# Retention and a SwiGLU block on one core: shorter tick queues, a later first split batch, narrower first weight loads

## The chip, the cores and the metric

The kernel runs on one core of one Trainium2 chip. A core has five engines with a queue each: TensorE (PE, matrix products; PEld is its weight load), VectorE (DVE), ScalarE (ACT), GpSimd (POOL) and SyncE (SP, which here only issues DMAs). Each engine takes its own queue in order; semaphores hold an instruction until what it needs is there. ScalarE's queue carries DMA issues too. The metric is the device time of one execution in microseconds; five executions of the kernel before were timed.

## What is computed

```python
scores = (q @ k^T) / sqrt(64)                      # batch 8, heads 8, sequence 576, head size 64
gamma  = 1 - 2 ** (-5 - h)                         # one decay per head h
ret    = scores * where(i >= j, gamma ** (i - j), 0)
x      = (ret @ v), laid out as 4608 tokens x 512  # heads side by side
g, val = x @ w_gate, x @ w_val                     # 512 -> 1536
out    = (silu(g) * val) @ w_out                   # 1536 -> 512
```

q, k and v are 32-bit floats. The three weight matrices are 64-bit floats in memory, so the kernel loads eight bytes per element and turns them into 32-bit floats itself.

## The kernel before

**Retention.** Two heads of one batch entry make a pair; there are 32 pairs, four per batch entry (HP = 4). The sequence of a pair is cut in nine chunks of 64. Within a chunk the masked scores are applied to v (`own_values`, L519); what earlier chunks contribute goes through a 64 x 64 state per chunk (`new_states`, L529; the decayed running sums in `masked`, L565 to L587) that the queries then read (`earlier_values`, L540 and L544). `to_x` moves the result to the token matrix.

**Ticks.** The pairs run as a software pipeline. `tick(t)` issues for pair t the transposes, for pair t-1 the scores (L552, L558), new states and masks, and for pair t-2 the two value steps and the move to x. TensorE's part of a tick is issued at once; what other engines do is put as small functions into a list `pieces`, and `part_on` hands one of them out at a time between the products of the feed-forward block. `go_on(len(pieces))` at the head of a tick hands out all that is left. For a light tick (decays folded into the queries in advance) the list of before is: `copies` with `outputs`; `own`; then `pairs`, `odd`, `evens`, one at a time; `keys` with the scaling of the queries; the transpose of the queries (qT); that of the keys (kT, both L483 on VectorE); and the next load.

**The first four pairs** (t = 0 to 3) are transposed on TensorE instead, against the identity matrix: for each of q and k four 128 x 128 transposes into a bank (L468) and, for the ninth chunk, two 64 x 64 transposes ("tails") into bankC (L470); two copies (L472, L473) bring them to SBUF, by VectorE for pair 0 and by ScalarE after it.

**Weights.** A weight load `load_w(m)` (L383, L385) brings a 1 MB block of 64-bit numbers into one of three places (RAWS = 3). `split(j)` makes two 32-bit parts of half a block on ScalarE (L402, L403), and issues a later `load_w` once both halves of a block are read; `rounding(j)` joins them on VectorE (L416, L417), and issues `split(j + 1)`.

**Feed-forward.** The first 512 tokens are computed directly: `up0` (L715) makes gate and value for one of 12 blocks of 128 hidden columns, `down0` (L727) the output. The other 4096 tokens are four tiles of 1024, each by a bilinear scheme with fewer block products: 3 x 26 `up_step`s (L941) and 26 `down_step`s (L982) per tile, with sums of operands before and of results after them (L749, L883, L911, L957 to L964). In the first of these tiles (n = 1) the weight sums are still being formed, on GpSimd and ScalarE, and each is stored to DRAM by a DMA on ScalarE's queue (L945); later tiles fetch them back, on SP (L844), into a ring of eight places. `up_step` hands out one piece where its result has fewer than five operations, `down_step` three.

**What sets the order.** The order on each engine is that of the Python program (a manual schedule); no planner changes it. In the 52 steps of n = 1 after its first 26, six ticks (12 to 17) are spread evenly by `merge`; four more lie in its 26 down steps.

Of the kernel before, what the change touches and what calls it, by code (L numbers as in the profile page):

```python
# [154 lines left out]
def kernel(  # L155
# [34 lines left out]
    B, H, S, D = q.shape  # L190
    NT, DM = out.shape
    DF = moe_w_gate.shape[1]
    P = 128
    HP = H // 2
# [3 lines left out]
    CW = NFULL * P  # L198
# [22 lines left out]
    bankA, bankB, bankC, bankE = banks = [ps.tile([P, 512], F32, name=n) for n in ("bankA", "bankB", "bankC", "bankE")]  # L221
# [138 lines left out]
    for u in range(NF // 2):  # L360
        for gv, w in enumerate((moe_w_gate, moe_w_val)):
            src = w[:, u * 2 * P : (u + 1) * 2 * P].rearrange("(c p) n -> p c n", p=P)
            weights.append((src, [w_up[:, u // 2, gv, 2 * (u % 2) + f].rearrange("p k x -> p (k x)") for f in range(2)]))
    NUP = len(weights)
    for u in range(NF // 2):
        src = moe_w_out[u * 2 * P : (u + 1) * 2 * P, :].rearrange("(f p) n -> p f n", p=P)
# [4 lines left out]
    RAWS = 3  # L371
    raws, parts = {}, {}

    def load_w(m, parts=range(2)):

        i, queue = order[m], nc.sync if m < 5 else nc.scalar
        raw = rest[:, raw_at + m % RAWS * 2048 : raw_at + (m % RAWS + 1) * 2048]
        raws[i] = raw.bitcast(I32)
        dst, src = raw.bitcast(I64), weights[i][0]
        if i < NUP:  # L380
            dst = dst.rearrange("p (c n) -> p c n", n=2 * P)
            for cols in [ts(f, P) for f in parts] if m < 2 else (slice(0, 2 * P),):
                queue.dma_start(out=dst[:, :, cols], in_=src[:, :, cols])  # L383
        else:
            queue.dma_start(out=dst.rearrange("p (f n) -> p f n", f=2), in_=src)  # L385
# [7 lines left out]
    def split(j):  # L393

        i, f = halves[j]
        bits = bits_of(i, f)
        top, ulp = [rest[:, part_at + 512 * (2 * n + j % 2) : part_at + 512 * (2 * n + j % 2 + 1)] for n in range(2)]  # L400
        blocks = lambda a: a.rearrange("p (c m) -> p c m", m=P)
        nc.scalar.activation(out=blocks(top), in_=bits[:, :, :, 1].bitcast(F32), func=AF.Prelu, scale=2.0 ** -112, alpha=2.0 ** 32)  # L402
        nc.scalar.activation(out=blocks(ulp.bitcast(I32)), in_=bits[:, :, :, 0].bitcast(U32), func=AF.Copy, scale=2.0 ** -29)  # L403
        parts[j] = top.bitcast(I32), ulp.bitcast(I32)
        m = j + 1 if 1 < j < 4 else j // 2 + RAWS
        if f and m < len(order):
            load_w(m)

    def rounding(j):

        i, f = halves[j]
        dst = weights[i][1][f].bitcast(I32)
        top, ulp = parts.pop(j)
        nc.vector.tensor_scalar(out=dst, in0=top, scalar1=3, scalar2=None, op0=ALU.logical_shift_left)  # L416
        nc.vector.tensor_tensor(out=dst, in0=dst, in1=ulp, op=ALU.add)  # L417
        if j + 1 < len(halves):
            split(j + 1)
# [36 lines left out]
    def transposes(i):  # L456
        p = i % HP
        qk, kn, vt = loaded.pop(i)
        qT = early[i] if i < HP else qp.tile([P, S], F32, tag="qT", name="qT")
        st[i] = dict(qT=qT, kn=kn, v=vt)  # L460
        pieces = []

        copy = nc.scalar.copy if i else nc.vector.tensor_copy
        if i < HP:

            for n, (t, src, bank) in enumerate(((kT, kn, bankB), (qT, qk, bankA)) if i else ((qT, qk, bankA), (kT, kn, bankB))):
                for c in range(NFULL):
                    nc.tensor.transpose(bank[:, ts(c, P)], src[:, ts(c, P)], ident)  # L468
                for hl in range(2):
                    nc.tensor.matmul(bankC[half[hl], ts(n, L)], src[half[hl], CW : CW + D], ident[half[hl], half[hl]],  # L470
                                     start=True, stop=True, skip_group_check=True)
                copy(t[:, 0:CW], bank)  # L472
                copy(t[:, CW:S], bankC[:, ts(n, L)])  # L473
        else:
            if light(i):
                def scale_q():

                    src = qk[:, 0].rearrange("p (j r) d -> p r j d", r=2)
                    for r in range(2):
                        nc.scalar.activation(out=src[:, r], in_=src[:, r], func=AF.Copy, scale=piece[:, 2 * p + r : 2 * p + r + 1])  # L480
                pieces.append(scale_q)
            for n, t in enumerate((qT, kT)):
                pieces.append(lambda n=n, t=t: nc.vector.transpose(out=t, in_=qk[:, n].rearrange("p j d -> p (j d)")))  # L483

        every = slice(0, P)

        def keys():
            blocks = kn.rearrange("p (g d) -> p g d", d=D)
            if i < HP:
                parts = [(0, every, blocks[:, 0 : NC - 1 : 2]), (1, every, blocks[:, 1:NC:2]), (1, half[1], blocks[half[1], NC - 1])]  # L490
            elif whole(i):
                parts = [(0, every, blocks[:, 0:NFULL]), (1, every, blocks[:, NFULL:NC])]
            else:
                parts = [(hl, every, blocks[:, hl : 2 * NFULL : 2]) for hl in range(2)]
            for hl, rows, at in parts:
                scale = key[rows, 2 * p + hl : 2 * p + hl + 1]
                if vector(i) or 1 < i < HP:
                    (nc.vector if vector(i) else nc.gpsimd).tensor_scalar(out=at, in0=at, scalar1=scale, scalar2=None, op0=ALU.mult)
                else:
                    nc.scalar.activation(out=at, in_=at, func=AF.Copy, scale=scale)  # L500

        if light(i):
            return [lambda: (keys(), pieces[0]())] + pieces[1:]
        return [keys] + pieces
# [138 lines left out]
    def tick(t, lo=HP, hi=NP, spread=False, then=None):  # L643
        go_on(len(pieces))
        if hi == HP:

            if lo <= t - 1 < hi:
                scores(t - 1, True)
                new_states(t - 1)
                pieces.extend(masked(t - 1))  # L650
                go_on(3)
            if t + 1 == HP:
                split(0)
                rounding(0)
            if lo <= t - 2 < hi:
                own_values(t - 2)
            for f in transposes(t) if lo <= t < hi else ():
                f()
            if t + 1 == HP:
                rounding(1)  # L660
            if lo <= t - 2 < hi:
                earlier_values(t - 2)
                to_x(t - 2)[0]()
            return
        if lo <= t - 2 < hi:
            own_values(t - 2)
        if lo <= t - 1 < hi:
            new_states(t - 1)
        if lo <= t - 2 < hi:
            earlier_values(t - 2)  # L670
        if lo <= t - 1 < hi:
            scores(t - 1, t - 2 < lo)
        if lo <= t - 1 < hi and whole(t - 2) and not whole(t - 1):
            decay(slice(0, H), slice(0, H), half[1])
        copies, *masks = masked(t - 1) if lo <= t - 1 < hi else (lambda: None,)
        keys, *new = transposes(t) if lo <= t < hi else (lambda: None,)
        outputs = to_x(t - 2)[0] if lo <= t - 2 < hi else lambda: None
        late = needed(1) - 4 <= t < needed(1) - 2 or light(t - 2)
        if late:
            pieces.append(lambda: (copies(), outputs()))  # L680
        else:
            pieces.extend([lambda: (copies(), keys()), outputs])
        pieces.extend(masks)
        if late:
            pieces.append(keys)
        pieces.extend(new)
        if then:
            pieces.append(then)
        if not spread:
            go_on(len(pieces))  # L690

# [18 lines left out]
    def up0(f, chunks):  # L710

        pair = banks[2 * (f % 2) : 2 * (f % 2) + 2]
        for gv, bank in enumerate(pair):
            for c in chunks:
                nc.tensor.matmul(bank, w_up[:, f // 4, gv, f % 4, c // 2, (c % 2) * P : (c % 2 + 1) * P], xs[0][:, c, :],  # L715
                                 start=(c == 0), stop=(c == HP - 1))
        if HP - 1 in chunks:
            s = io[:, (f % 2) * T0 : (f % 2 + 1) * T0]
            nc.scalar.activation(out=s, in_=pair[0], func=AF.Silu)
            nc.vector.tensor_tensor(out=hid0[f], in0=pair[1], in1=s, op=ALU.mult)  # L720
# [288 lines left out]
    for t in range(HP + 2):  # L1009
        tick(t, 0, HP)  # L1010

        if t == 3:
            load(HP)
        for j in {3: (2, 3), 5: (4, 5)}.get(t, ()):
            rounding(j)
        if 3 <= t <= 4:
            up0(t - 3, range(2))
    for f in range(2):
        up0(f, range(2, HP))
    load(HP + 1)  # L1020


# [113 lines left out]
```

## Time and profile before

| What | Value |
|---|---|
| Median of five runs | 1060.25 us (1058.42 to 1063.54) |
| The profiled execution, its own time | 1057.86 us |
| Its span, first to last instruction | 1056.1 us |
| TensorE busy | 1035.4 us (98%) |
| VectorE busy | 648.5 us (61%) |
| ScalarE busy | 284.9 us (27%) |
| GpSimd busy | 392.8 us (37%) |
| Moved by DMA | 199.09 MB, 189 GB/s on average |

The profile is of one execution. A row of the timeline gives start, duration, engine, line, operation, what is written and read, and in brackets how long the engine stood idle before it and what ended that. A row of waits gives the waiting engine with its tile and line, what released it, the total in us, how often, and the longest. A row of stretches gives, after the times from and to, the length and then the busy time of TensorE, its weight load, VectorE, ScalarE and GpSimd, each with its number of instructions, then the granted share of TensorE's clock, the share of the DMA engines' time in use, and GB/s. The early retention pairs and the first 512 tokens take up to about 180 us, the first large tile lies from 180 to about 420, and the three others follow.

### The profile page before, as it was taken

Reading aid. Unit: us, or ns where it says so; the run is one execution under the profiler, and the core shown is the slowest. Engines: PE = TensorE matmul, PEld = TensorE weight load, DVE = VectorE, ACT = ScalarE, POOL = GpSimd, SP = SyncE. Lnnn points to the kernel's source line nnn. Section 1 sums busy time; section 2 is a strip of 40 time slices with the busy share of each in tenths; the row PEclk is TensorE's granted clock in tenths of the full one; section 3 lists DMA queues with packets and bytes.
Section 4 is the critical chain, followed back from the end, with each engine's and each line's share of the span. In section 5 each row is a group of like instructions: output and inputs, shape, how many; then the busy total and the mean of one; then the engine's idle time right before and its main releaser. Section 6 shows DMA issues by size and latency. Waiting matters only on the chain.

```text
span 1056.1 us, 21447 instructions
## 1 busy us (share of the span) xinstructions
PE 1035.4 (98%) x8448; PEld 851.9 (81%) x8448; DVE 648.5 (61%) x1063; ACT 284.9 (27%) x610; POOL 392.8 (37%) x338
## 2 busy tenths in 40 slices
PE   7999999989999999999999999999999999999998
PEld 5554555878887888888888888888888888888887
DVE  5568786866758767454467787526375654244644
ACT  4555422243443310331312112232220022232110
POOL 3002367666455207622224038412250383122505
PEclk9999999999999999999999999999999999999999
DMA  9998777665777888756766777545554565555653
GB/s 262 246 261 252 186 203 268 174 203 168 181 205 219 214 227 227 217 149 179 192 173 190 209 197 213 154 143 150 150 175 150 155 189 150 153 155 159 181 160 99
DMA packets 305083, 199.09 MB, mean 189 GB/s; under 512 B 219992, under 2 KB 248664, under 8 KB 304984
## 3 DMA queue, kind: packets, MB, share of 16 engines
q1 hardware_dynamic: 273848, 161.64, 56.5%
q10 hardware_dynamic: 31136, 36.08, 10.1%
q8 instruction: 67, 1.10, 0.4%
q14 instruction: 32, 0.26, 0.1%
HBM read 157.56 MB, written 40.11 MB: 187 GB/s over the span
## 4 chain that ended last, share of the span: by engine, by line
PE 92%; DVE 4%; DMA 2%; issue 1%; ACT 0%; ACTq 0%; POOL 0%; DVEq 0%; SPq 0%
PE bankC L941 12%; PE bankA L941 12%; PE bankE L941 12%; PE bankB L941 11%; PE bankB L982 6%; PE bankC L982 6%; PE bankA L982 6%; PE bankE L982 6%; PE bankA L715 2%; PE bankC L715 2%; PE outer L544 2%; PE bankB L715 2%; PE bankE L715 2%; PE outer L519 2%; DVE rest L883 2%; PE inner L558 2%
## 5 line engine op out<-in xcount | busy, mean ns | idle before, releaser
L883 POOL TENSOR_TENSOR rest<-rest 128x512 f32<-128x512 f32 x56 | 79.4, 1423 | 293.6 <-DVE rest L883 275.2
L957 ACT ACTIVATE io<-rest 128x256 f32<-128x256 f32 x180 | 75.0, 416 | 337.3 <-DVE rest L883 289.4
L941 PE MATMUL bankC<-rest,arena 128*128 128x256 f32 x544 | 129.1, 380 | 1.0 <-DVE rest L883 1.0
L941 PE MATMUL bankA<-rest,arena 128*128 128x256 f32 x544 | 128.7, 380 | 0.0
L749 POOL TENSOR_TENSOR arena<-arena 128x512 f32<-128x512 f32 (+1 forms) x72 | 114.3, 1599 | 31.2 <-DMA up<-arena 14.7
L941 PE MATMUL bankE<-rest,arena 128*128 128x256 f32 x512 | 121.4, 380 | 0.6 <-DVE rest L883 0.6
L941 PE MATMUL bankB<-rest,arena 128*128 128x256 f32 x512 | 121.2, 380 | 0.0
L941 PEld LDWEIGHTS bankC<-rest,arena 128*128 128x128 f32 x544 | 102.9, 190 | 15.5 <-issue 1.3
L941 PEld LDWEIGHTS bankA<-rest,arena 128*128 128x128 f32 x544 | 103.3, 190 | 14.4 <-issue 0.5
L964 POOL TENSOR_TENSOR arena<-rest,io 128x256 f32<-128x256 f32 x72 | 51.9, 726 | 166.4 <-ACT io L957 166.4
L941 PEld LDWEIGHTS bankE<-rest,arena 128*128 128x128 f32 x512 | 97.0, 190 | 14.1 <-issue 0.9
L941 PEld LDWEIGHTS bankB<-rest,arena 128*128 128x128 f32 x512 | 97.2, 190 | 13.2
L749 POOL TENSOR_TENSOR rest<-rest 128x256 f32<-128x256 f32 (+1 forms) x66 | 67.5, 1042 | 100.5 <-DVE rest L417 59.6
L883 DVE TENSOR_TENSOR rest<-bankA,rest 128x512 f32<-128x512 f32 x72 | 48.9, 688 | 72.7 <-PE bankA L941 55.2
L883 DVE TENSOR_TENSOR rest<-bankC,rest 128x512 f32<-128x512 f32 x72 | 48.9, 687 | 67.0 <-PE bankC L941 45.2
L883 DVE TENSOR_TENSOR rest<-bankE,rest 128x512 f32<-128x512 f32 x72 | 48.8, 686 | 64.4 <-PE bankE L941 47.0
L883 DVE TENSOR_TENSOR rest<-bankB,rest 128x512 f32<-128x512 f32 x72 | 48.7, 685 | 62.4 <-PE bankB L941 44.6
L960 DVE SCALAR_TENSOR_TENSOR arena<-rest,io 128x256 f32<-128x256 f32 x84 | 57.2, 684 | 11.8 <-ACT io L957 11.3
L982 PE MATMUL bankB<-arena 128*128 128x256 f32 x252 | 58.3, 381 | 0.0
L982 PE MATMUL bankA<-arena 128*128 128x256 f32 x252 | 58.0, 380 | 0.3 <-DMA arena<-dn 0.3
L982 PE MATMUL bankC<-arena 128*128 128x256 f32 x252 | 58.1, 380 | 0.0
L982 PE MATMUL bankE<-arena 128*128 128x256 f32 x252 | 57.9, 380 | 0.0
(184 smaller groups left out, 1628.1 us busy)
## 6 DMA issues: line engine op xcount, KB each, us to landing
arena<-up SPq DMA_DIRECT2D x234, 256.0 KB, 2.7
arena<-dn SPq DMA_DIRECT2D x104, 384.0 KB, 3.6
up<-arena ACTq DMA_DIRECT2D x78, 256.0 KB, 2.6
dn<-rest SPq DMA_DIRECT2D x78, 128.0 KB, 1.8
out_dram<-rest SPq DMA_DIRECT2D x32, 256.0 KB, 3.3
qk<-in_q_dram SPq DMA_DIRECT2D x108, 72.0 KB, 3.0
qk<-in_k_dram SPq DMA_DIRECT2D x108, 72.0 KB, 2.4
rest<-in_moe_w_out_dram ACTq DMA_DIRECT2D x6, 1024.0 KB, 5.8
```

What stands on the lines that cost most here:

```text
L519: m = nc.tensor.matmul(xo[half[hl ^ r * exchange(i)], c, r], s["v"][rows, at], ret[rows, r if whole(i) else hl, c], start=(c == 0), stop=( ...
L544: nc.tensor.matmul(xr[half[hl]] if c + 1 == NC else xo[half[hl ^ c % 2 * exchange(i)], c // 2, c % 2], state[half[hl], c, :], s["qT"][half ...
L558: nc.tensor.matmul(sc[chunk(i, hl, 2 * c + r)[0], r if whole(i) else hl, c], kT[half[hl], at], qT[half[hl], at], start=True, stop=True, sk ...
L715: nc.tensor.matmul(bank, w_up[:, f // 4, gv, f % 4, c // 2, (c % 2) * P : (c % 2 + 1) * P], xs[0][:, c, :], start=(c == 0), stop=(c == HP ...
L749: eng.tensor_tensor(out=dst, in0=srcs[0], in1=srcs[1], op=ALU.add if op[0] == "add" else ALU.subtract)
L883: eng.tensor_tensor(out=at(op[1]), in0=at(op[2]), in1=at(op[3]), op=ALU.add if op[0] == "add" else ALU.subtract)
L941: m = nc.tensor.matmul(b[:, gv * TB : (gv + 1) * TB], w[:, gv, ts(c, P)], rhs[:, c, :], start=(opens and gv == 0 and c == 0), stop=(c == 1 ...
L957: nc.scalar.activation(out=s, in_=src[:, 0:TB], func=AF.Silu, scale=-1.0 if negative else 1.0)
L960: return lambda: nc.vector.scalar_tensor_tensor(out=dst, in0=src[:, TB : 2 * TB], scalar=-1.0, in1=s, op0=ALU.mult, op1=ALU.mult)
L964: nc.gpsimd.tensor_tensor(out=dst, in0=src[:, TB : 2 * TB], in1=s, op=ALU.mult)
L982: nc.tensor.matmul(b[:, m * TB : (m + 1) * TB], lhs[:, qd, ts(m, P)], w[:, qd], start=(opens and qd == 0 and m == 0), stop=(qd == NQ - 1), ...
```

## The change

Four edits, which leave every arithmetic operation as it is:

1. Each of the first three weight blocks is loaded by 64 columns at a time: twelve DMAs of 256 KB instead of four of 512 KB and one of 1 MB.
2. For the first four pairs both groups of 128-wide transposes come first, each followed by its copy, then the tails of k and q, then the copies of the tails.
3. `split(0)` and `rounding(0)` go behind the fourth pair's transposes (and behind `own_values` of the second pair); `rounding(1)` goes behind the load of pair 4, `rounding(2)` and `rounding(3)` one tick later, and the first half of the first two `up0` products becomes one batch at the end of tick 4, the second half one at the end of tick 5.
4. In light ticks `own` joins `copies` and `outputs`, and `keys` joins `evens`; in all spread ticks the next load joins the last transpose. A light tick then has six pieces.

```diff
-            for cols in [ts(f, P) for f in parts] if m < 2 else (slice(0, 2 * P),):
+            for cols in [ts(2 * f + n, D) for f in parts for n in range(2)] if m < RAWS else [slice(0, 2 * P)]:
                 queue.dma_start(out=dst[:, :, cols], in_=src[:, :, cols])
...
-            for n, (t, src, bank) in enumerate(((kT, kn, bankB), (qT, qk, bankA)) if i else ((qT, qk, bankA), (kT, kn, bankB))):
+            for t, src, bank in ((kT, kn, bankB), (qT, qk, bankA)) if i else ((qT, qk, bankA), (kT, kn, bankB)):
                 for c in range(NFULL):
                     nc.tensor.transpose(bank[:, ts(c, P)], src[:, ts(c, P)], ident)
+                copy(t[:, 0:CW], bank)
+            tails = ((kT, kn), (qT, qk))
+            for n, (_, src) in enumerate(tails):
                 for hl in range(2):
                     nc.tensor.matmul(bankC[half[hl], ts(n, L)], src[half[hl], CW : CW + D], ident[half[hl], half[hl]],
                                      start=True, stop=True, skip_group_check=True)
-                copy(t[:, 0:CW], bank)
+            for n, (t, _) in enumerate(tails):
                 copy(t[:, CW:S], bankC[:, ts(n, L)])
...
-            if t + 1 == HP:
-                split(0)
-                rounding(0)
             if lo <= t - 2 < hi:
                 own_values(t - 2)
             for f in transposes(t) if lo <= t < hi else ():
                 f()
             if t + 1 == HP:
-                rounding(1)
+                split(0)
+                rounding(0)
...
-        if late:
-            pieces.append(lambda: (copies(), outputs()))
+        if late and masks:
+            own, (pairs, odd, evens) = masks
+            pieces.extend([lambda: (copies(), outputs(), own()), [pairs, odd, lambda: (evens(), keys())]])
+        elif late:
+            pieces.append(lambda: (copies(), outputs(), keys()))
         else:
             pieces.extend([lambda: (copies(), keys()), outputs])
-        pieces.extend(masks)
-        if late:
-            pieces.append(keys)
-        pieces.extend(new)
-        if then:
-            pieces.append(then)
+            pieces.extend(masks)
+        if then and new:
+            pieces.extend(new[:-1])
+            pieces.append(lambda: (new[-1](), then()))
+        else:
+            pieces.extend(new)
+            pieces.extend([then] if then else [])
...
-        for j in {3: (2, 3), 5: (4, 5)}.get(t, ()):
+        for j in {3: (1,), 4: (2, 3), 5: (4, 5)}.get(t, ()):
             rounding(j)
-        if 3 <= t <= 4:
-            up0(t - 3, range(2))
-    for f in range(2):
-        up0(f, range(2, HP))
+        for f in range(2):
+            if t > 3:
+                up0(f, range(2) if t == 4 else range(2, HP))
     load(HP + 1)
```

## The prediction

> **What bounds the kernel now.** I read the page's busy shares first, then whom TensorE waited for, then the stretches, then the order of time around each wait.
>
> ```profile
> PE 1035.4 (98%) x8448; PEld 851.9 (81%) x8448; DVE 648.5 (61%) x1063; ACT 284.9 (27%) x610; POOL 392.8 (37%) x338
> ```
>
> TensorE is busy for 98% of the span. Only its idle time, 1056.1 - 1035.4 = 20.7 us, can be won by reordering.
>
> ```profile
> PE outer L552 <- DVE kT L483: 5.5, 3, 2.0
> PE bankA L468 <- DMA qk<-in_q_dram: 4.7, 1, 4.7
> PE bankA L941 <- POOL arena L911: 1.8, 1, 1.8
> PE bankC L470 <- ACT kT L473: 1.1, 1, 1.1
> PE bankC L941 <- DVE rest L883: 1.0, 1, 1.0
> ...
> PE bankE L552 <- DVE kT L473: 0.5, 1, 0.5
> PE bankE L552 <- ACT rest L473: 0.4, 1, 0.4
> ```
>
> These are TensorE's waits (total, times, longest). The first load (4.7) is untouched. The change aims at the first row (three scores that waited for the transposed keys) and at the rows with L473 (copies of the early transposes).
>
> ```profile
> 259.76 1.49 DVE L963 TENSOR_TENSOR arena<-rest,io 128x256 f32<-128x256 f32 x1
> ...
> 261.18 0.77 DVE L483 STREAM_TRANSPOSE qT<-qk 128x576 f32<-128x576 f32 x1
> 261.87 0.65 DVE L883 TENSOR_TENSOR rest<-bankB,rest 128x512 f32<-128x512 f32 x1
> 262.45 0.75 DVE L483 STREAM_TRANSPOSE kT<-qk 128x576 f32<-128x576 f32 x1
> ...
> 263.25 0.27 PE L552 MATMUL outer<-qT,kT 64*64 64x64 f32 x2 [1.74 <-DVE kT L483]
> ```
>
> This is the timeline at the first of the three: the two transposes stand late in VectorE's queue, behind five pieces of evacuation work (from 257.70), and the next tick's scores are there first. The others, in the same view, are at 283.89 (1.97) and 321.01 (1.74). All three lie in second-tile gate/value products (up_step, n = 1), where six ticks share 52 products.
>
> ```profile
> 24.12 0.22 ACT L473 COPY kT<-bankC 128x64 f32<-128x64 f32 x1
> ...
> 24.38 0.69 DVE L417 CUSTOM_DVE_ANT_0 arena<-arena,rest 128x1024 uint16<-128x1024 uint16 x1
> 24.40 0.33 PE L470 MATMUL bankC<-ident,rest 64*64 64x64 f32 x4 [1.08 <-ACT kT L473]
> ...
> 27.09 1.12 PE L715 MATMUL bankA<-rest,arena 128*128 128x512 f32 x2 [0.25 <-DVE rest L616]
> ```
>
> At the fourth pair the second tail transpose (L470) waits 1.08 for a copy that stood behind two splits on ScalarE.
>
> **Part 1, tails and first batch.** The instructions are the same, reordered. Both 128-wide transposes go first, then both tails, then the copies. For pairs 0 and 1 this lets one copy run under the other tail: about 0.1 us each (of the 0.5 and 0.4 above). For the fourth pair I count from 21.88, where own_values(1) ends in the chain. TensorE: transposes 0.60 + 0.59, tails 0.6, earlier_values(1) 0.33 + 0.93, scores 0.55, new states 0.47: 26.0. The next step, own_values(2), overwrites `outer`, so it needs to_x(1). On VectorE that now stands behind rounding(0) alone, but split(0) stands behind the copies on ScalarE: tails copied at 24.05, split(0) to 25.25 (two rows of 0.6), second rounding instruction 0.69 to 25.95, to_x(1) 0.97 to 26.9. So 0.9 of the 1.08 comes back as a new wait. Then own_values(2) and earlier_values(2) 1.85 to 28.75, and the first two product groups 2 x 1.72 to 32.2. The third needs rounding(2), queued behind rounding(1) (to 28.0), masks and states (2.5) and to_x(2) (0.9): 31.4 + 1.06 = 32.45. Products to 35.9; own_values(3) and earlier_values(3) 1.93: 37.85. In the trace of before this point is 38.56. Saved: 0.7. Bounds: TensorE's idle time after the first load is 2.7 us up to 50 us, so at most +2.7; if VectorE's chain is 1.7 longer than worked out, -1.
>
> A rule speaks on these gaps: the Trainium skill, "TensorE: Matmul & The Clock Gate", section "What's actually happening", has the array start at half clock and warm after about 3.4 us of sustained work in a free-running window. The row: four transposes take 1.11 us until 13 us and 0.67 from 16.66 on. By the rule fuller early work could warm it one window sooner (an estimate: 3.4 us of half-speed work, so -1.7), or a new gap later; by the row the step comes at 16.66 again, 0. The granted clock reads 1.00 throughout the stretches, so it doesn't decide; I take 0.
>
> **Part 2, six pieces per tick.** In light ticks the order was copies+outputs, own, pairs, odd, evens, keys (with the query scale), qT, kT, load: nine steps. Now it is copies+outputs+own, pairs, odd, evens+keys, qT, kT+load: six. One goes out per product step of fewer than five operations; 52/6 = 8.7 product steps a tick, so nine spill over into the next tick's start and six don't. In VectorE's new order kT stands five instructions earlier at the first wait: before the `rest<-bankC` add that ran at 257.70. With evens ending near 255.7 and the query scale done near 255.5 (ScalarE was idle 253.7 to 256.7, so keys 0.95 and scale 0.95 fit there), kT ends near 257.7; the scores come at 261.5. Saved: 1.74. The third wait has the same pattern (ScalarE idle 311.4 to 314.5): 1.74. At the second, keys and scale stand ahead of ScalarE's w_sums instruction (L910) and two `io` silus, 1.9 us that lay behind them; VectorE's L963 there waits for them and for a store. kT then ends near 281.5 instead of 283.8, with everything 1.7 earlier after the first saving: 279.8 against scores at 280.1. I take 1.5 of 1.97 (0 to 1.97). `ret` moves into time when VectorE idles (2.81 us before 266.01 and before 323.77). Sum: 5.0, bounds 1.7 to 5.5. Cover: VectorE is 98% busy from 270 to 280; if this is what paces the stretch, the second saving is lost.
>
> **Part 3, loads moved with kT.** Each tick's load, eight quarter DMAs and kn and v, leaves SP one to four fetches earlier. The built program gives DMAs eight completion semaphores in turn, so one waits for the eighth before it. The one tight place is the last up tick: load(19) went behind nine `arena<-dn` fetches, now behind five. On SP that load took 344.55 to 354.42, 9.9 us; five fetches from 332.67 at 1.3 each end at 339.2; so the sixth is issued near 349.1 and lands 3.6 to 5.0 later, 352.7 to 354.1. TensorE wants it at 353.9 (the sixth `L982` group in the chain). Cost 0.2 by this, up to 3 if kT or a semaphore holds the load; I take 0.8. Later tiles have no wait of TensorE at all after 345, and their ring holds eight steps (13.8 us) against a 10 us load: 0.
>
> **Part 4, weights by 64 columns.** Five DMAs (4 x 512 KB, 1 MB) become twelve of 256 KB. SP: seven more issues x 0.51 = 3.6 us. Engines, from the two queues' rows:
>
> ```profile
> q1 hardware_dynamic: 273848, 161.64, 56.5%
> q10 hardware_dynamic: 31136, 36.08, 10.1%
> ```
>
> 56.5% and 10.1% of 16 x 1056 us are 34.9 ns for a 590 B packet and 54.8 for 1158 B, so about 14 ns + 0.035 per byte: 32, 50 and 86 ns for 512, 1024 and 2048 B. Extra: (4096 x 32 - 2048 x 50)/16 ns = 1.8 and (2048 x 32 - 512 x 86)/16 ns = 1.3: 3.1 us.
>
> ```profile
> 0.00:25.00 25.00, 18.04 (x384) 14.68 (x386) 12.05 (x34) 10.05 (x24) 7.33 (x17) 1.00 1.00 260
> ```
>
> The DMA engines are full there (share 1.00), so these 3.1 us delay what follows. Cover: split(0), (1) and (4) ran at 21.13, 22.53 and 28.13, when their data was there, and now can't start before 24.05, 25.2 and 32.5: slack 2.9, 2.7 and 4.4. The fourth weight also goes behind load(4) on SP, as rounding(1) moved behind it; it lands near 40 instead of 31 to 35. Its split ran at 39.87; ScalarE then has a table load and the first silu (42.58), which must be done by 45.7, when the product that reuses bankA starts: 2.5 us of cover, then 1:1. The rule against: the Trainium skill, "DMA: Bandwidth & Descriptors", "Rules for kernel authors" asks for 1 MiB or more per DMA, and its section on the anatomy of one DMA gives about 2.0 us fixed each. Seven more would be 14 us if they came one after the other; by the full stretch above they overlap. I take 0, bounds 0 to 10 (rival C).
>
> **Sum.** 0.7 + 5.0 - 0.8 - 0 = 4.9 us off a span of 1056.1. That execution took 1057.86, 1.8 outside the span; the median of the five runs is 1060.25, 2.4 above it. I take the same saving from the median: 1055.4.
>
> **The rivals.** A measurement here can tell about 0.3%, 3.2 us: below 1057.1 is faster, above 1063.4 slower.
> A, as summed: 1055.4, own range 1052.5 (all three waits and 2.3 of the start) to 1057. For it: TensorE has no work but waits at these places, and little waits elsewhere afterwards.
> B, the waits move: VectorE and ScalarE set the pace from 267 to 284 and from 328 to 345, so one saving (1.7) survives or the sixth fetch is 3 late: 1.7 to 3.1 saved, 1058. For it: the 98% above and the chain's many L883 steps; against it: VectorE idles 2.8 us before both stretches. Here the change doesn't do what its six pieces say.
> C, slower: the fourth weight is late. Place: split(6) ahead of the first silu. With 2 us per extra DMA it lands at 40 + 14 = 54; past the cover (43) each us costs one: 11 lost against 4.9 won, 1066. It decides from a landing at 51 on (8 us lost). Against it: full engines.
>
> **How the numbers follow.** A 0.60, B 0.24, C 0.16 (with lesser losses at the start in it, a third of which end within 0.3%). A ends faster but for a few in a hundred, which B's lucky end gives back: faster 0.60, same 0.27, slower 0.13. Range 1052 to 1062: it leaves out 0.04 below and about 0.14 of C above.
>
> **What would show it.** TensorE's row `L552 <- DVE kT` gone or under 0.5; `bankC L470 <- ACT kT` gone, with about 0.9 before own_values(2) (L519) near 26; TensorE without idle time from about 38; tile two's first down product near 333 instead of 337.8. I am wrong if `L982` waits for `arena<-dn` by over 1 us, if splits wait for weight DMAs while TensorE idles between 38 and 60, or if new waits on L883 appear from 230 to 340.

## The result: no change that can be measured, and the profile after

| | median | executions |
|---|---|---|
| before | 1059.87 us (1055.51 to 1063.88) | 71 |
| after | 1060.68 us (1056.53 to 1063.20) | 36 |

The ratio is 1.0006, with a 95% interval of 0.9998 to 1.0014: 0.8 us more, where 4.9 less were forecast. The time lies inside the range (1052 to 1062), but in its upper part, where the prediction had put the other cases. The profiled execution of after took 1062.54 us, 4.7 more than that of before; it is one of the longer ones of its kernel, so its waits show the mechanism, not the typical sum.

The busy shares of after, and TensorE's waits (waiting engine with tile and line, releaser, total us, times, longest; the lines of the changed kernel are numbered 3 to 6 higher):

```profile
PE 1036.1 (98%) x8448; PEld 851.0 (80%) x8448; DVE 654.8 (62%) x1063; ACT 283.7 (27%) x610; POOL 393.1 (37%) x338
...
PE bankA L468 <- DMA qk<-in_q_dram: 5.1, 1, 5.1
PE bankA L720 <- ACT io L724: 4.7, 1, 4.7
PE bankC L946 <- POOL arena L916: 2.0, 1, 2.0
PE bankE L946 <- POOL arena L916: 1.9, 1, 1.9
PE outer L522 <- DVE arena L416: 1.1, 1, 1.1
```

TensorE does the same work (1036.1 us against 1035.4). What the change aimed at is gone: no row names kT any more (5.5 before), nor `bankC L470` (1.1). In their place stand three rows that before did not have: 4.7 on the first silu, and twice 2.0 on GpSimd's weight sums. The row `L522 <- DVE arena L416`, 1.1, is the wait of own_values(2) that the prediction had at 0.9.

Against before, from the two lists: kT 5.5, `bankC L470` 1.1 and the sum at 212 (1.8, now 0.25) are 8.1 us less; 4.7 + 2.0 + 1.9 + 1.1 on the new waits and 0.6 on `L522 <- issue` are 10.3 more, the first load 0.4; and two stretches of 3.4 us ran at half clock (0.6 of the first still inside the wait), 3.1 us more. That is 5.7, against the 4.7 by which the spans differ. TensorE came to full clock at 11.1 us instead of 16.7, which works the other way; how much it is worth was not measured, and small waits are left out of the sum.

Of the prediction's own signs of being wrong one came: splits wait for weight DMAs while TensorE idles between 38 and 60 us. The first down product of the large tile stands at 341.18, where 333 was forecast and 337.83 was before.

The first silu, in the timeline of before and then in that of after (start, duration, engine, line, operation, what is written and read; in brackets the idle time before it and what ended it):

```profile
26.17 0.37 SPq L383 DMA_DIRECT2D rest<-in_moe_w_val_dram  x1
...
39.87 0.68 ACT L402 ACTIVATE rest<-rest 128x512 f32<-128x512 f32 x1 [7.16 <-DVE arena L416]
...
42.58 0.60 ACT L719 ACTIVATE io<-bankA 128x512 f32<-128x512 f32 x1
```

```profile
33.86 1.94 SPq L383 DMA_DIRECT2D rest<-in_moe_w_val_dram  x1
...
46.04 0.66 ACT L402 ACTIVATE rest<-rest 128x512 f32<-128x512 f32 x1 [12.58 <-DMA rest<-in_moe_w_val_dram]
...
47.26 1.28 ACT L724 ACT_TABLE_LOAD   x1
...
48.56 0.60 ACT L724 ACTIVATE io<-bankA 128x512 f32<-128x512 f32 x1
```

The fourth weight is asked for at 33.86 (at 26.17 before) and lands 12.2 us later, at 46. ScalarE's queue stands for 12.58 us in front of its split, and the table load and the silu lie behind that split: 48.56 instead of 42.58. TensorE, which is at bankA again at 44.55, stands until 49.21.

The place in the first large tile, in the same view, before and after:

```profile
274.88 0.61 ACT L910 ACTIVATE arena<-arena 128x512 f32<-128x512 f32 x1
...
275.58 1.27 POOL L911 TENSOR_TENSOR arena<-arena 128x512 f32<-128x512 f32 x1 [6.87 <-ACT arena L910]
...
276.92 0.95 ACT L500 ACTIVATE kn<-kn,tab 128x256 f32<-128x256 f32 x2
```

```profile
278.61 0.95 ACT L503 ACTIVATE kn<-kn,tab 128x256 f32<-128x256 f32 x2
...
279.46 0.95 ACT L483 ACTIVATE qk<-qk,tab 128x288 f32<-128x288 f32 x2
...
280.31 0.61 ACT L915 ACTIVATE arena<-arena 128x512 f32<-128x512 f32 x1
...
281.00 1.27 POOL L916 TENSOR_TENSOR arena<-arena 128x512 f32<-128x512 f32 x1 [7.71 <-ACT arena L915]
...
282.32 1.99 PE L946 MATMUL bankC<-x_odd,arena 128*128 128x256 f32 x8 [2.02 <-POOL arena L916]
```

Before, the negation (L910) ran at 274.88, and the scaling of the keys behind it at 276.92. Now keys and query scale (1.7 us from 278.61) stand in front of the negation (L915 in the changed kernel) in ScalarE's queue. GpSimd has been idle for 7.71 us waiting for that negation, where it was 6.87 before; its sum takes 1.27, and the product that reads the sum is 2.02 late. The same pattern is at 336.84, 1.95 late: the keys at 334.45 now precede the negation at 336.15; before they followed it (334.68 behind 332.64).

### The profile page after: what moved, and what is told of

Read it like the earlier page. It is cut to its first block, busy times and chain, and to the rows that moved or that the text cites. A ratio compares the mean times of both kernels' runs of the same rounds, so it can differ in the third digit from the quotient of the medians.

```text
span 1060.8 us, 21467 instructions
## 1 busy us (share of the span) xinstructions
PE 1036.1 (98%) x8448; PEld 851.0 (80%) x8448; DVE 654.8 (62%) x1063; ACT 283.7 (27%) x610; POOL 393.1 (37%) x338
## 3 DMA queue, kind: packets, MB, share of 16 engines
q1 hardware_dynamic: 277544, 161.65, 56.3%
## 4 chain that ended last, share of the span: by engine, by line
PE 87%; DVE 4%; issue 2%; DMA 1%; POOL 1%; ACT 1%; SPq 1%; ACTq 0%; DVEq 0%; POOLq 0%
PE bankC L946 11%; PE bankA L946 11%; PE bankE L946 11%; PE bankB L946 11%; PE bankA L987 6%; PE bankB L987 6%; PE bankC L987 6%; PE bankE L987 6%; PE bankA L720 2%; PE outer L547 2%; PE outer L522 2%; PE bankC L720 2%; PE bankB L720 2%; PE bankE L720 2%; DVE rest L888 2%
```

## Experiments

Two theories stood after this. **Theory 1**: the fourth weight is late, because its request (issued by the split behind rounding(1)) moved behind the load of pair 4. **Theory 2**: `keys` in the piece of the evens puts ScalarE's scalings ahead of the negations that GpSimd's weight sums need. The rival of both is B of the prediction: other engines set the pace of the first large tile, and waits removed in one place come back in another. A third reason to be weighed was the narrow columns by themselves (C's fixed price per DMA). The expectations number them in two ways: in those of the fourth weight and of the wide columns Theory 2 is the narrow columns, and in those of the six pieces and of keys with queries Theory 3 is `keys`; later ones number as here. Runs of before that were made along with the experiments had medians of 1059.5 to 1059.8; each ratio is to those of its own series.

**The fourth weight ahead of load 4** (to the changed kernel):

```diff
         if t == 3:
+            rounding(1)
             load(HP)
-        for j in {3: (1,), 4: (2, 3), 5: (4, 5)}.get(t, ()):
+        for j in {4: (2, 3), 5: (4, 5)}.get(t, ()):
```

> The changed kernel with one line moved: rounding(1), and with it the fourth weight's load, stands ahead of the load of pair 4 again. Theory 1 (the place in SP's queue makes the fourth weight late, and this holds the first silu): the fourth weight is issued near 26 instead of 33.9 and lands by 38; TensorE's wait of 4.7 us for the first silu (L720 after L724) falls below 0.5, and the half-clock window near 48.6 goes; time 1060.7 - 4.7 - 1.5 = about 1055 us, faster than before by 0.3 to 0.5%. Theory 2 (the twelve narrow DMAs make it late, wherever it stands): the wait stays over 3 us and the time stays at 1060 to 1061.

Measured: 1056.47 us, ratio 0.9966 (0.9950 to 0.9981), 4.2 below after, where some 6 were expected from one profile of after, one of its longer executions. `load` only issues DMAs on SP, so this edit changes the order of that queue alone. The timeline of this kernel at the same place:

```profile
25.86 0.37 SPq L383 DMA_DIRECT2D rest<-in_moe_w_val_dram  x1
...
37.63 0.69 ACT L402 ACTIVATE rest<-rest 128x512 f32<-128x512 f32 x1 [5.13 <-DVE arena L416]
...
39.16 1.28 ACT L724 ACT_TABLE_LOAD   x1
...
40.46 0.60 ACT L724 ACTIVATE io<-bankA 128x512 f32<-128x512 f32 x1
```

The request is back at 25.86; the split is held by a rounding now, not by a DMA; the silu is done before TensorE needs it at 43.43. The wait of 4.7 is gone, and the two of 2.0 on GpSimd are still there (2.0 and 1.9). Theory 1 holds for the start, in this order of the columns; the next run limits it.

**Wide columns in the changed kernel**: edit 1 undone, all else as in after.

```diff
-            for cols in [ts(2 * f + n, D) for f in parts for n in range(2)] if m < RAWS else [slice(0, 2 * P)]:
+            for cols in [ts(f, P) for f in parts] if m < 2 else (slice(0, 2 * P),):
```

> The changed kernel with the first three weights in their five wide DMAs, and the fourth still behind the load of pair 4. Theory 1 (the place in the queue): the five DMAs save 3.1 us of the engines' time and 3.6 us of SP issue at most, so the wait for the first silu shrinks from 4.7 to between 1.5 and 4.7 but does not go; time 1058 to 1061. Theory 2 (the narrow DMAs): the wait goes, time about 1055.

Measured: 1059.15 us, 0.9988 (0.9976 to 1.0000), 1.5 below after. Here the load of pair 4 starts on SP at 19.98 instead of 26.40. Its last request is out at 32.31, and the fourth weight, asked for at 32.41, is read at 40.92: no wait on the silu. But own_values(2) waits 2.0 (`L522 <- DVE arena L417`). So neither expectation fits whole: the wait went, and the time stayed. The late request alone is not enough in this execution.

The packets tell what differs. In both kernels SP's queue moves the keys and values of pair 4 before the fourth weight, and the last of these is asked for 0.7 us before it. In after another weight (the sixth) was asked for on ScalarE's queue at 33.49, ahead of the fourth. From 33.8 to 38 it took 0.58 of the 1.13 MB that moved. SP's queue moved only packets under 512 B in that time, where those of the fourth weight have 2 KB; the first of these moved near 38.8. With wide columns the sixth was asked for at 34.31, behind the fourth: from 32.4 to 36 SP's queue moved 0.86 of 0.87 MB, and the fourth weight's packets began near 34.5. The wait on the silu thus needs the late request and what moves beside it; why the order of these two requests turned, in one profile of each, was not tested.

**The six pieces alone** (edit 4 on the kernel before; its diff is that part of the change):

> The kernel before with the six pieces per tick alone. Theory 3 (keys and query scale now stand ahead of ScalarE's negation for a weight sum, so GpSimd's sum and TensorE's product wait for it): the three waits for the transposed keys (5.5 us) are gone, two waits of about 2 us each on GpSimd's weight sum stand near 280 and 336, the earlier one of 1.8 near 213 may shrink; net 1 to 3 us saved, 1057 to 1059, not told from before. Rival (the six pieces are worth what was predicted, and GpSimd waited only because the start was late): no wait of TensorE over 1 us from 230 to 345, time about 1055.

Measured: 1059.06 us, 0.9991 (0.9980 to 1.0002). TensorE's waits:

```profile
PE bankA L468 <- DMA qk<-in_q_dram: 4.3, 1, 4.3
PE bankC L945 <- POOL arena L915: 2.0, 1, 2.0
PE bankE L945 <- POOL arena L915: 2.0, 1, 2.0
PE outer L519 <- issue: 1.4, 1, 1.4
PE bankC L945 <- DVE rest L887: 1.0, 1, 1.0
```

All three waits on kT are gone, and two of 2.0 have come: with the start of before, too. The edit that was to win 4.2 with its loads won 0.6, which can't be told from nothing; the time is at the upper end of what Theory 3 of the expectation gave (1057 to 1059).

**Keys with the queries** (to the changed kernel):

```diff
-            pieces.extend([lambda: (copies(), outputs(), own()), [pairs, odd, lambda: (evens(), keys())]])
+            pieces.extend([lambda: (copies(), outputs(), own()), [pairs, odd, evens]])
+            if new:
+                new[0] = lambda first=new[0]: (keys(), first())
+            else:
+                pieces.append(keys)
```

There are still six pieces; keys and query scale come one piece later.

> The changed kernel with keys and query scale taken from the piece of evens and put in front of the query transpose, one product step later; still six pieces. Theory 3: on ScalarE they now stand behind both negations of that step, so GpSimd's sums come 1.9 us earlier and TensorE's waits near 280 and 336 (2.0 and 1.95) go or fall below 0.7, with at most 1 us of waiting for the transposed keys in their place; with the half-clock window near 339 gone too, 4 to 5 us less than the changed kernel, about 1056. The start, with its wait of 4.7, is as in the changed kernel. Rival (GpSimd is late for another reason, such as its own 3.9 us of sums or a store it waits for): the waits on GpSimd stay within 0.5 us, time 1060 to 1061.

Measured: 1057.37 us, 0.9971 (0.9959 to 0.9984), 3.3 below after. TensorE's waits between 200 and 400 us:

```profile
PE bankC L950 <- DVE rest L892: 1.3, 1, 1.3
PE bankE L950 <- DVE rest L892: 1.1, 2, 0.6
PE bankA L950 <- DVE rest L892: 0.7, 1, 0.7
PE bankB L950 <- POOL arena L920: 0.5, 1, 0.5
PE bankC L950 <- POOL arena L920: 0.4, 1, 0.4
PE bankE L950 <- POOL arena L920: 0.4, 1, 0.4
```

In the timeline the negation now runs at 275.20, ahead of the keys at 276.55, the sum at 275.89, and the product waits 0.40 instead of 2.02; the second place, 0.40 instead of 1.95. No wait on kT came back. Theory 2 holds; its rival, another reason for GpSimd's lateness, falls. The wait on the first silu is still there, 2.0 in this execution: with the same order at the start it was 4.7 in the profile of after.

**Both mendings**, run in two series:

> The changed kernel with both mendings: the fourth weight asked for ahead of the load of pair 4, and keys with the query scale in the piece of qT instead of that of the evens. Theory 1 (the fourth weight's landing) priced the first mending at 4.2 us by medians (1060.7 to 1056.5), theory 2 (the negations of L915 queued behind keys and query scale on ScalarE) the second at 3.3 (1060.7 to 1057.4). If the two causes are separate, as they lie 230 us apart and on different engines, the savings add: 1053.2, with no wait of TensorE above 1.3 us after the first load. Rival: what is won at the start is lost again before 345 us, because stores and GpSimd's weight sums set the pace of the first large tile and not TensorE: then 1056, with waits on L888 or L916 growing by 2 or more.

> The kernel with both mendings once more, unchanged, since its first time rests on five executions: 1053.7 again within 0.8, and below the 1055.5 of its twin with wide columns if the narrow columns are worth anything in this order; if the difference between the twins was chance, 1054.5 or more.

Measured: 1053.73 us, 0.9953 (0.9937 to 0.9970), and 1054.17 us, 0.9952 (0.9937 to 0.9967). The two savings add within the noise, as causes far apart should (1053.2 expected); no wait after the first load is above 1.5 us in either profile. This version is 0.5% faster than the kernel before, and 0.6% faster than the changed one.

**The same with wide columns**:

> As the run with both mendings, but the first three weight blocks in five wide DMAs, as in the kernel before. If narrow columns themselves delay transfers (eight places for DMAs in flight, more issues on SP), this is 1 to 2 us faster than with them: 1051.5. If they bring the first halves of the weights in time for the first two roundings, this is about 1 us slower: the wait of own_values(2) near 25 us is 2.0 by L417, as in the run of the changed kernel with wide columns, against 0.65: 1054.2. If both weigh nothing once the fourth weight is early: 1053.2.

Measured: 1055.50 us, 0.9969 (0.9958 to 0.9980). Its median is 1.3 to 1.8 above the twin's, the side on which narrow columns help, and by more than the 1 us expected; the intervals still overlap. Its profile has own_values(2) 1.4 late on `arena L416` (in the twin 0.8, there behind L619, and 1.0), and 2.2 on `L522 <- issue`, a row that most other profiles have too, at 0.3 to 1.4. So the first wait is in line with the expectation, and how much of the rest is the columns is open.

**The start alone** (edits 1 to 3 without the six pieces):

> Edits 1 to 3 without the six pieces. Theory 1: the start alone costs what the changed kernel loses against the run with six pieces only, 1060.7 - 1059.1 = 1.6: 1061.2 against 1059.6 before; the second use of bankA waits 2 to 4.7 us for the first silu, and the fourth weight lands 10 us or more after its issue. The three waits on kT and the one on GpSimd near 212 stand as in the kernel before. Rival (the start's edits lose nothing by themselves, the loss needs the new pieces): 1058.6, the 1.28 us that the fourth pair's stretch gained, and no wait on the first silu.

Measured: 1061.18 us, 1.0023 (1.0011 to 1.0035). The profiled execution is the longest of the 22 (1067.80), so its waits are not the typical ones. TensorE's longest:

```profile
PE outer L555 <- DVE kT L486: 5.5, 3, 2.0
PE bankA L468 <- POOL near L343: 4.3, 1, 4.3
PE bankA L716 <- ACT io L720: 4.1, 1, 4.1
PE bankA L942 <- POOL arena L912: 2.8, 1, 2.8
```

The loss at the start needs no new pieces: the wait on the silu is there (4.1), the three on kT are untouched. The rival of that expectation (1058.6) falls.

**The columns alone** (edit 1 on the kernel before):

> The kernel before with edit 1 alone: twelve DMAs of 256 KB for the first three weight blocks, everything else as it was, so the fourth weight is still asked for ahead of the load of pair 4. A fixed price of 2 us for each of seven more DMAs (rival C of the prediction) would give 14 less the 5 of cover that the splits have: 1068. What the prediction took, nothing, gives 1059.6; the start of load 4 on SP then moves from 26.6 to 28 to 29. Between, 1061.5, if only the DMA engines' 3.1 us of extra work pass into the first silu, which has 2.5 us of cover.

Measured: 1060.19 us, 1.0003 (0.9989 to 1.0017), 0.4 above before. Fourteen us from seven more DMAs, or the 9 of them that the cover leaves, are excluded. How they can cost something in this order is in the timeline of the profiled execution, the longest of the thirteen (1063.55):

```profile
24.54 0.66 ACT L402 ACTIVATE rest<-rest 128x512 f32<-128x512 f32 x1 [1.45 <-DMA rest<-in_moe_w_val_dram]
...
26.13 0.22 ACT L473 COPY kT<-bankC 128x64 f32<-128x64 f32 x1
...
26.40 0.48 PE L470 MATMUL bankC<-ident,rest 64*64 64x64 f32 x4 [3.85 <-ACT kT L473]
```

Two splits wait for their columns (2.43 and 1.45), the copies of the fourth pair stand behind them on ScalarE, and the tail waits 3.85 (1.08 before). As the median is only 0.4 up, most executions can't have lost that much. In the changed kernel the splits stand behind those copies, and its profile has no such row: edit 3 is what gives the columns their slack there.

**The mended pieces alone** (the kernel before with the pieces as in the run with keys and queries together):

> The kernel before with the pieces of a tick alone changed, and keys with the query scale kept in the piece of qT: the order at the start is that of the kernel before. Theory 2 (the second wait went over to GpSimd's weight sums because the negations stood behind keys and query scale): the three waits on kT (5.5) and the one near 212 (1.8, of which 0.4 to 0.8 stays) are gone and nothing of 2 us comes in their place; at the six pieces only's 1059.1 the two new waits of 2.0 are missing, less some 0.5 to 1.0 of new small ones on L892: 1056.0. Rival (the six pieces win nothing whatever their order, and what the mending won was only worth anything after the late weight): 1058.6 or more, the time of the kernel before less what lies within 0.1%.

Measured: 1055.18 us, 0.9961 (0.9947 to 0.9975). Nothing of 2 us is left in its waits:

```profile
PE bankA L468 <- DMA qk<-in_q_dram: 4.2, 1, 4.2
PE bankC L470 <- ACT kT L473: 1.3, 1, 1.3
PE bankC L949 <- DVE rest L891: 1.0, 1, 1.0
PE bankE L949 <- DVE rest L891: 0.9, 2, 0.6
```

The rival (1058.6 or more) falls. Against the 1059.06 of the six pieces alone, the place of `keys` is worth 3.9 us.

## Why the prediction was wrong

Two terms carry it. The medians of the runs split the forecast so; each difference is uncertain by 1 to 2 us, so that the parts meet the sum of +0.8 exactly is luck, and the start's gain beside the mended pieces is barely told from nothing:

| | forecast | as changed | mended |
|---|---|---|---|
| ticks: Parts 2 and 3 | -5.0 + 0.8 = -4.2 | -0.6 (1059.06 - 1059.62) | -4.4 (1055.18 - 1059.54) |
| start: Parts 1 and 4 | -0.7 | +1.4 (1061.18 - 1059.76) | -2.6 (1056.47 - 1059.06) beside the six pieces, -1.5 and -1.0 (1053.73 and 1054.17 - 1055.18) beside the mended ones |
| sum | -4.9 | +0.8 (measured for both together: +0.8) | -6.0 (1053.73 - 1059.76) and -5.4 (1054.17 - 1059.54) |

**Part 2, the second wait: the step that failed.** The prediction saw that keys and query scale would stand ahead of L910's negations, "1.9 us that lay behind them", and followed those 1.9 us along one reader only, VectorE's additions and kT. The other reader is GpSimd, whose sum waits for the negation alone and feeds a product of TensorE. There it cost 2.02, which the prediction had put at nothing. It cost 1.95 once more one tick after the third wait, where no wait on kT had stood and of which the prediction says nothing. The forecast that kT comes in time was right at all three places. With `keys` one piece later the gain is there, 4.4 (2.6 to 5.6) against the 4.2 forecast; that it comes so close is in part luck, since the 0.8 set aside for loads was not lost and the wait near 212, in no term of the forecast, is 0.5 in that profile. This is rival B in its outcome (the waits move), with another cause than B gave: not VectorE's pace, but the order in ScalarE's queue, since the mended pieces have the same work on VectorE.

**Part 4: "it lands near 40", then "I take 0".** It landed at 46.0 in the profile. The place and the chain behind it were as rival C had them (split(6), table load, first silu, bankA), and so was the rule of 1:1 past the cover: the silu came 6.0 us later than before, and TensorE waited 4.7 in this execution, 4.1 and 2.0 in two others with the same start. (The cover was 1.3, not 2.5: TensorE was back at bankA at 44.55, 1.1 earlier than the 45.66 before.) What was mis-sized is the landing time: the prediction counted the place in SP's queue and not what stood ahead of the block and moved beside it. It was 12.2 us from the request, while the end of load 4, three weight blocks (asked for at 33.49, 33.86 and 35.89) and the beginning of load 5 shared the engines; about 5 of them had gone before its first packets moved, near 38.8. And C's price was wrong in the other direction. The Trainium skill, "DMA: Bandwidth & Descriptors", in its section on the anatomy of one DMA, gives about 2.0 us fixed for each DMA on the path from GpSimd, while these are issued by SyncE; seven more DMAs by themselves cost 0.4 (-1.2 to +1.8, the run with the columns alone), so they overlap. The engines' extra work, worked out as 3.1 us, does not show in the queue totals either:

```profile
q1 hardware_dynamic: 277544, 161.65, 56.3%
q10 hardware_dynamic: 31136, 36.08, 10.1%
```

There are 3696 more packets, but 56.3% of 1060.8 is 597.2 us against 56.5% of 1056.1, 596.7: 0.5 more, with 0.5 of rounding on each.

**Part 1** was right in its mechanism: the L470 wait is gone, and own_values(2) waits in its place (0.9 forecast, 1.05 measured, at 25.65). The values of the fourth pair's stretch end at 37.28 instead of 38.56, a gain of 1.28 where 0.7 was taken. A part of the difference is the clock, which the prediction had put at 0: the array was at full speed from 11.1 us in this execution. It was so from 16.7 or 17.1 in before and in three more profiles, and from 11.0 to 12.4 in seven others, with old and new starts in both groups and the kernel with both mendings once in each (16.7 and 11.0), so this goes by the execution, not by the change. The granted clock of 1.00 that the prediction read for the first stretch said nothing on it: the clock records of that profile begin at 16.7.

**Part 3** was right that nothing breaks: no wait of TensorE on `arena<-dn` is left, where 0.3 stood before and 0.8 was set aside.

**The sum against the median.** The prediction took the saving from a profile of before, where the waits on kT are the same in every profile with the old pieces (5.5 in three of three). The GpSimd wait near 212 is not: 1.8, 2.8 and 0.4 with the old pieces. So its 1.5 in the comparison of the two profiles need not be the change's.

## What to carry to other kernels

When a piece of work is moved forward in an in-order queue, list every instruction that it passes, and for each of them every engine that reads its result; the delay can go to each reader, and an engine that idles because its input is late (GpSimd, 7.71 us) has no slack, however idle it looks. When a request for data is moved behind another load, cost not the time of its issue but that of its landing with everything that is then in flight. And where an edit wins less than its removed wait, look for a wait of nearly the same length elsewhere before giving the edit up: here moving one call by one piece brought the 4 us back.

## What the runs showed of the hardware

Short waits cost TensorE more than their length. Products of the same kind after the 4.66 us wait, and two stretches around the wait of 1.95 (columns: from and to, length, busy time of TensorE, its weight load, VectorE, ScalarE, GpSimd, granted clock, share of the DMA engines, GB/s), in the profile of after:

```profile
330.00:338.00 8.00, 6.21 (x29) 5.11 (x27) 7.04 (x17) 3.63 (x9) 1.16 (x1) 1.00 0.82 293
338.00:343.00 5.00, 4.84 (x15) 3.98 (x16) 3.02 (x6) 0.83 (x2) 2.46 (x3) 0.66 0.96 284
```

```profile
49.21 5.09 PE L720 MATMUL bankA<-rest,arena 128*128 128x512 f32 x8 [4.66 <-ACT io L724]
...
54.14 3.60 PE L720 MATMUL bankB<-rest,arena 128*128 128x512 f32 x8
```

The eight products after the wait take 5.09 us, eight of the same form later 3.60. The clock records have windows of 3.41 us, or two of them, at half speed, which begin up to 1.6 us after a wait has ended, or within it where it is longest. Over all profiles of this study, for waits of TensorE after it had warmed up: of twelve of 1.37 to 1.78 us none was followed by such a window, of thirteen of 1.93 to 2.04 six, and all five of 2.19 or more. A window costs up to 1.7 us (3.41 at half speed), so a wait of 2 us costs nearly 3 on average, by this estimate from six of thirteen. This can be a part of what the mendings won over after, whose profile has two windows: both profiles of the kernel with both mendings have none. The profile of before has none either.

The Trainium skill, "TensorE: Matmul & The Clock Gate", section "What's actually happening", has the array go cold after an idle window of about 3.4 us that runs freely. A wait of 2 us is shorter than that, and a window followed it in about half of the cases: the same wait of 2.02 on the same product was followed by one in the run with the six pieces alone, and not in after. That it goes by chance fits a free-running window, but the bound here lies near 2 us, not 3.4.

The landing time of a 1 MB block at the start was not a property of the block: 12.2 us after its request in the profile of after, and in the run with keys and queries together, with the same order on SP, 10.5 (32.63 to 43.16). The wait on the silu followed it, 4.7 and 2.0.
